# Start-up and step order of a fused FFT filter and gated FFN kernel: x on all partitions, interleaved filter rows, one table tensor, gated loads, written order, stages B and C in separate steps

## The chip, the core and the metric

The kernel runs on one core of one Trainium2 chip. The metric is the time of one execution in device microseconds (us). Three times of the kernel before were given: 1010.28, 1011.1 and 1007.79 us. Executions agree within about 0.3%, so an effect of 2 or 3 us is read only from several runs or from the trace itself.

## The reference

x is 8 batches of 3008 rows of 256 values. Each batch gets a real FFT along its 3008 rows, a product with a complex filter and the inverse FFT. Then all 24064 rows go through an FFN.

```python
X = np.fft.rfft(x, axis=1)
y = np.fft.irfft(X * (filt_r + 1j * filt_i)[None], n=3008, axis=1)
y = y.reshape(24064, 256)
out = (np.maximum(y @ w_gate, 0) * (y @ w_val)) @ w_out      # d_ff = 1536
```

## The kernel before

3008 is split as 94 times 32. Each batch's FFT is done in three stages of matmuls, with a transposition through DRAM between them:

- Stage A: the 94-point transform, an fp32 matmul (psA), copied to asb and stored in a DRAM tensor Abuf.
- Stage B: Abuf is loaded as at; a 32-point transform (psX), two products with the filter on VectorE (tt, uu), the inverse 32-point transform (psD), copied to dsb and stored in Dbuf.
- Stage C: Dbuf is loaded as dC; the inverse 94-point transform (psY), copied to yT.

The FFN then works on blocks of 376 rows. A block has 12 steps (ft 0 to 11). A step does four matmuls of 376 columns (psV, psG), ScalarE copies psV (vsb), VectorE multiplies (prod), and three matmuls of 256 columns (psO) use the products of the block before. FFT stages of the next batch are put into FFN steps as "side" work, so that TensorE never stops. There psX, psD and psY share two buffers of the accumulation memory, called banks below. Only batch 0's FFT has no FFN beside it; this document calls that time the start-up, up to the first psV matmul. The rest, from the first psV matmul to the last psO matmul, is called the FFN phase.

The parts that the change touches (cuts are marked):

```python
def load_x(b, eng):
    for c in range(N2 // NC2):                       # 4 tiles of 94 partitions
        xf = sb.tile([N1, NC2 * D], FP32, tag="xf", bufs=4)
        for (p0, p1) in ((0, 80), (80, N1)):
            eng.dma_start(xf[p0:p1], ...)
...
def hold_gpsimd(tile_):                              # a gate: GpSimd's next loads wait for tile_
    scr = sb.tile([32, 8], BF16, tag="scr", bufs=1)
    nc.gpsimd.tensor_copy(scr, tile_)
...
nc.sync.dma_start(WA, ...); load_x(0, nc.sync)
load_filters(); load_tables(); load_vg(0)
warm(20)                                             # warm-up: matmuls on constants, result not used
for i, f in enumerate(items_a(0)):
    f(); warm(1)
    if i == 7: place_tables(0)
load_at(0); place_filters(0)
for i, f in enumerate(items_b(0, after)):            # after: at g == 10, gate, load_vg(1), load_vg(2)
    if i == 4: place_tables(H); place_filters(1)     # copies on VectorE
    f()
load_d(0); hold_gpsimd(dCs[0, 0][0:32, 0, 0:8]); load_o(); load_x(1, nc.gpsimd)
...
for i, f in enumerate(items_a(b + 1)): side.setdefault(20 + (3 * i) // 2, []).append(f)
side.setdefault(45, []).append(lambda b=b: load_at(b + 1))
side.setdefault(46, []).append(lambda b=b: load_x(b + 2, nc.gpsimd))
for i, f in enumerate(items_b(b + 1)): side.setdefault(56 + (7 * i) // 4, []).append(f)
side.setdefault(79, []).append(lambda b=b: load_d(b + 1))
...
if ft in (5, 8) and bi + 1 < len(blocks):            # stage C of the next block
    item_c(*blocks[bi + 1], 0 if ft == 5 else 1)
```

This is the order in which the program is written. The kernel before leaves the final order of each engine's instructions to a scheduler.

## Time and profile before

| | value | from |
|---|---|---|
| timed runs | 1007.79 to 1011.1 us | three runs |
| span of the profiled execution | 3590.8 us | page, first line |
| TensorE busy | 99% | page, part 1 |
| start of psV, psG, psO groups | every 1.25 us (2 x 376 or 3 x 256 columns) | timeline |

The profiled execution is 3.6 times as long as the timed ones. The page's head (span and instructions; then each engine's busy time, share and instructions):

```profile
span 3590.8 us, 18213 instructions
...
PE 3561.6 (99%) x6756; PEld 1532.6 (43%) x6756; DVE 601.8 (17%) x1062; ACT 581.3 (16%) x1177; POOL 48.5 (1%) x92
```

And three neighbouring groups of the timeline (start, busy time, engine and line, operation, output and inputs, count):

```profile
1010.34 1.57 PE L326 MATMUL psV<-yT,WvT 128*128 128x376 bf16 x2
...
1011.59 1.57 PE L326 MATMUL psG<-yT,WgT 128*128 128x376 bf16 x2
...
1012.85 1.42 PE L346 MATMUL psO<-WoT,prod 128*128 128x256 bf16 x3
```

Two matmuls of 376 columns take 1.25 us from start to start, and three of 256 take 1.26 us. That is about 600 columns per microsecond. TensorE's rate should be 2400 by the Trainium skill (TensorE: Matmul & The Clock Gate, Part 1), so this one execution ran at about a quarter of it, though the granted clock is given as 1.00. (The trace of this execution holds no entry for the clock at all; so the 1.00 means only that nothing was recorded.) On such a slow TensorE all other engines look idle, and almost every wait is hidden. This profile can be used for durations on the other engines and for orders, but not for the balance of the timed runs. A second thing can be read from it: GpSimd's queue issues all six loads of gate and value weights from 30.2 to 34.5 us, and the copy that was meant to gate the last four comes at 119 us. The scheduler has put the loads before their gate. The first of the four:

```profile
31.65 0.72 POOL L202 DMA_DIRECT2D WvT<-in_moe_w_val_dram  x1
```

And the copy, further on in the same timeline:

```profile
118.94 0.18 POOL L214 COPY scr<-dsb 32x8 bf16<-32x8 bf16 x1 [73.39 <-ACT dsb L279]
```

VectorE's costs are read from the groups of the same page: 550 ns for one prod, 692 for a tt and 681 for a uu.

### The profile page before, as it was taken

What the parts mean: (1) busy time and instruction counts of PE and PEld (TensorE: products, weight loads), DVE (VectorE), ACT (ScalarE), POOL (GpSimd) and SP (SyncE); (2) the same over time, 40 slices, a digit from 0 to 9 for tenths busy, and PEclk for the clock granted to TensorE, in tenths of its full rate; (3) what the DMA queues carried; (4) which work ended last, traced back from release to release, by engine and by line L of the source; (5) the groups of instructions that cost most, each with busy time, mean ns of one, the idle gap of its engine ahead of it and who ended that gap; (6) DMA issues with size and microseconds to landing.
All of it is one profiled execution on the core that took longest, in us unless ns stands there. A gap on an engine that the chain in (4) does not pass through costs nothing.

```text
span 3590.8 us, 18213 instructions
## 1 busy us (share of the span) xinstructions
PE 3561.6 (99%) x6756; PEld 1532.6 (43%) x6756; DVE 601.8 (17%) x1062; ACT 581.3 (16%) x1177; POOL 48.5 (1%) x92
## 2 busy tenths in 40 slices
PE   8899999999999999999999999999999999999999
PEld 2333444344443344433444344443444434444444
DVE  2311221112211121111211112110121101211111
ACT  0111111111111111111111111111111111111111
POOL 2000000000000000000000000000000000000000
DMA  6302010110101101001010110101101001010000
GB/s 113 83 21 62 16 33 9 33 49 16 32 9 33 49 17 35 9 30 49 19 33 9 32 51 19 31 7 40 43 19 31 9 18 29 19 31 9 9 9 13
DMA packets 95226, 105.94 MB, mean 30 GB/s; under 512 B 5920, under 2 KB 85984, under 8 KB 92128
## 3 DMA queue, kind: packets, MB, share of 16 engines
q1 hardware_dynamic: 83984, 78.11, 7.5%
q0 software_dynamic: 10176, 25.47, 3.0%
q10 hardware_dynamic: 976, 1.20, 0.2%
q8 instruction: 53, 0.87, 0.1%
q14 instruction: 37, 0.30, 0.0%
HBM read 58.84 MB, written 49.81 MB: 30 GB/s over the span
## 4 chain that ended last, share of the span: by engine, by line
PE 99%; DMA 1%; ACT 0%; DVE 0%; issue 0%; SPq 0%
PE psO L346 26%; PE psV L326 26%; PE psG L326 26%; PE psA L230 12%; PE psX L263 2%; PE psD L277 2%; PE psD L276 2%; PE psY L309 2%; PE psJ L369 1%; DMA xf<-in_x_dram 0%; DMA dC<-Dbuf_74 0%; DMA at<-Abuf_66 0%; DMA WA<-dft_wa 0%; DMA Abuf_66<-asb 0%; DMA Dbuf_74<-dsb 0%; DVE asb L234 0%
## 5 line engine op out<-in xcount | busy, mean ns | idle before, releaser
L346 PE MATMUL psO<-WoT,prod 128*128 128x256 bf16 (+1 forms) x2304 | 1162.4, 692 | 0.0
L326 PE MATMUL psV<-yT,WvT 128*128 128x376 bf16 x1536 | 1144.3, 887 | 0.0
L326 PE MATMUL psG<-yT,WgT 128*128 128x376 bf16 x1536 | 1143.3, 883 | 0.0
L331 DVE SCALAR_TENSOR_TENSOR prod<-psG,vsb 128x376 bf16<-128x376 f32 x768 | 422.1, 550 | 2606.2 <-PE psG L326 2604.2
L346 PEld LDWEIGHTS <-prod 128*128 128x128 bf16 (+1 forms) x2304 | 533.8, 232 | 703.2 <-issue 675.6
L329 ACT CAST vsb<-psV 128x376 bf16<-128x376 f32 x768 | 362.7, 472 | 1630.3 <-PE psV L326 1630.3
L326 PEld LDWEIGHTS <-WgT 128*128 128x128 bf16 x1536 | 341.2, 222 | 584.1 <-issue 584.1
L326 PEld LDWEIGHTS <-WvT 128*128 128x128 bf16 x1536 | 332.1, 221 | 433.8 <-issue 418.2
L230 PE MATMUL psA<-xf,WA 94*96 94x512 f32 x256 | 455.9, 1927 | 11.5 <-DMA xf<-in_x_dram 11.5
L236 ACT CAST asb<-psA 96x512 bf16<-96x512 f32 x120 | 69.8, 582 | 635.5 <-PE psA L230 635.5
L309 PEld LDWEIGHTS <-dC 96*128 96x128 bf16 x512 | 95.2, 216 | 119.6 <-issue 107.9
L277 PE MATMUL psD<-uu,I2u 128*128 128x256 bf16 x192 | 134.3, 699 | 0.0
L276 PE MATMUL psD<-tt,I2t 128*128 128x256 bf16 x192 | 134.0, 698 | 0.0
L230 PEld LDWEIGHTS psA<-xf,WA 94*96 94x96 f32 x256 | 102.6, 413 | 61.5 <-issue 43.0
L309 PE MATMUL psY<-M_83,dC 96*128 96x94 bf16 x512 | 113.4, 425 | 7.1 <-DMA dC<-Dbuf_74 7.1
L279 ACT CAST dsb<-psD 128x512 bf16<-128x512 f32 x96 | 56.3, 586 | 360.5 <-PE psD L277 360.5
L263 PE MATMUL psX<-at,F_84 128*128 128x256 bf16 x192 | 105.1, 692 | 7.3 <-DMA at<-Abuf_66 7.3
L351 ACT COPY osb<-psO 128x512 f32<-128x512 f32 (+1 forms) x128 | 61.3, 479 | 261.3 <-PE psO L346 261.3
L266 DVE TENSOR_TENSOR tt<-psX,Ftr 128x512 bf16<-128x512 f32 x96 | 66.4, 692 | 147.6 <-PE psX L263 139.1
L267 DVE TENSOR_TENSOR uu<-psX,Fti 128x512 bf16<-128x512 f32 x96 | 65.4, 681 | 0.0
L141 POOL DMA_DIRECT2D xf<-in_x_dram x56 | 29.8, 537 | 2390.6 <-PE psA L230 2389.7
L263 PEld LDWEIGHTS <-F_84 128*128 128x128 bf16 x192 | 40.7, 212 | 48.9 <-issue 34.9
(38 smaller groups left out, 236.2 us busy)
## 6 DMA issues: line engine op xcount, KB each, us to landing
xf<-in_x_dram POOLq DMA_DIRECT2D x28, 640.0 KB, 5.5
out_dram<-osb SPq DMA_DIRECT2D x64, 256.0 KB, 2.2
out_dram<-osb SPq DMA_DIRECT2D x64, 120.0 KB
xf<-in_x_dram POOLq DMA_DIRECT2D x28, 112.0 KB, 5.9
xf<-in_x_dram SPq DMA_DIRECT2D x4, 640.0 KB, 10.5
Abuf_66<-asb SPq DMA_DIRECT2D x4, 384.0 KB, 4.4
at<-Abuf_66 SPq DMA_DIRECT2D x4, 384.0 KB, 4.5
Dbuf_74<-dsb SPq DMA_DIRECT2D x4, 384.0 KB, 3.4
```

The source lines that it names most:

```text
L230: nc.tensor.matmul(psA[0:NROW], WA, xf[:, j * 512:(j + 1) * 512], start=True, stop=True)
L236: nc.scalar.copy(dst, psA[0:NROW])
L263: nc.tensor.matmul(psX[:, i], F2[:, g + i, :], at[:, g + i, :], start=True, stop=True)
L266: nc.vector.tensor_tensor(tt, psX, Ftr[:, g:g + 2, :], op=ALU.mult)
L267: nc.vector.tensor_tensor(uu, psX, Fti[:, g:g + 2, :], op=ALU.mult)
L276: nc.tensor.matmul(psD[:, i], I2t[:, g + i, :], tt[:, i], start=True, stop=False)
L277: nc.tensor.matmul(psD[:, i], I2u[:, g + i, :], uu[:, i], start=False, stop=True)
L309: nc.tensor.matmul(psY[:, j * N1:(j + 1) * N1], dCs[b, z // 2][:, (z % 2) * 4 + j, h * 128:(h + 1) * 128], M1, start=True, stop=True)
L326: nc.tensor.matmul(pt[:, :W], w[:, h, ft * 128:(ft + 1) * 128], yt[:, h, :], start=(h == 0), stop=(h == 1))
L329: nc.scalar.copy(vsb, psV[:, :W])
L331: nc.vector.scalar_tensor_tensor(prod, in0=psG[:, :W], scalar=0.0, in1=vsb, op0=ALU.max, op1=ALU.mult)
L346: nc.tensor.matmul(psO[:tw, t % 2], prods[ft][:, t * 128:t * 128 + tw], WoT[:, ft, :], start=(ft == 0), stop=(ft == NFT - 1))
```

## The change

The intent: give x the DMA engines alone at the start and spread it over all partitions; load filters, tables and weights only when a gate opens; keep the written order so that the gates hold; take copies off VectorE in the first stage B; shorten the last store and load before stage C; and keep stages B and C in different FFN steps. The diff, cut to its core:

```diff
+    ctx.enter_context(tc.manual_schedule())          # each engine keeps the written order
-    WA = consts.tile([N1, NROW], FP32)
+    WA = consts.tile([128, NROW], FP32)              # row n1 on partition 4 * (n1 % 32) + n1 // 32
+    XF = [consts.tile([128, NX2 * D], FP32, name=f"XF{c}") for c in range(N2 // NX2)]   # NX2 = 16
...
     def load_x(b, eng):
-            for (p0, p1) in ((0, 80), (80, N1)):
-                eng.dma_start(xf[p0:p1], ...)
+            for m in range(3):
+                eng.dma_start(xf[m:m + 4 * rows - 3:4], ...)      # 32 rows, every fourth partition
...                                                    # filter rows: dst[r:r+31:2] and dst[r+1:r+32:2]
...                                                    # three tables in one tensor, two DMAs, issued in stage A
+                if half == 0: nc.vector.tensor_copy(dst[r + 32:r + 64, gs, :], dst[r:r + 32, gs, :])
+                else:         nc.sync.dma_start(dst[r + 32:r + 64, gs, :], dst[r:r + 32, gs, :])
...
+        cuts = (0, 6, 12, 18, 24) if b else (0, 6, 12, 18, 22, 24)   # stores of dsb
-                if g: inv()
+                if len(held) > 2: inv()                # tt, uu, dsb: 4 buffers
...                                                    # dC: eight loads of 4 columns, not four of 8
-    load_filters(); load_tables(); load_vg(0)
+    (zero XF on VectorE and GpSimd); load_x(0, nc.sync)
+    hold_gpsimd(XF[0][0:32, 0:8]); load_filters(0); load_filters(1)
+    warm(16)
+    (stage A, with load_tables() after its third item)
+    load_at(0); place_tables(0, nc.vector.tensor_copy); place_tables(1, nc.scalar.copy)
+    place_filters(0); place_filters(1)
+    hold_gpsimd(ats[0][0:32, NG - 1, 0:8]); load_vg(0); load_vg(1); load_vg(2)
+    (stage B with two warm-up matmuls per item); warm(16); load_d(0)
...
+            s0 = 5 if b else 20                        # side work: A at s0, at load at s0 + 25, x at s0 + 26
-                side.setdefault(56 + (7 * i) // 4, []).append(f)
+                at_step(s0 + 36 + (3 * i) // 2, f)
-            if ft in (5, 8) and bi + 1 < len(blocks):
+            if ft in (7, 10) and bi + 1 < len(blocks):
```

More of the change, by code (lines that the diff above doesn't have):

```diff
@@ L40, in _tables @@
     p = np.arange(16)
-    wa = np.zeros((N1, NROW))
+    wa = np.zeros((128, NROW))
+    part = 4 * (n1 % 32) + n1 // 32
     m1 = np.zeros((NROW, N1))
@@ L55, in _tables @@
         th = 2 * np.pi * ((n1 * k1) % N1) / N1
-        wa[:, 2 * hg] = np.cos(th)
+        wa[part, 2 * hg] = np.cos(th)
         if k1 not in (0, 47):
-            wa[:, 2 * hg + 1] = -np.sin(th)
+            wa[part, 2 * hg + 1] = -np.sin(th)
             m1[2 * hg] = 2.0 * np.cos(th) / S
             m1[2 * hg + 1] = -2.0 * np.sin(th) / S
-            k = np.concatenate([k1 + N1 * p, S - (N1 * (p + 1) - k1)])
-            conj = np.concatenate([np.ones(16), -np.ones(16)])
+            k = np.stack([k1 + N1 * p, S - (N1 * (p + 1) - k1)], 1).reshape(32)
+            conj = np.tile([1.0, -1.0], 16)
             th = 2 * np.pi * (np.outer(n2, k) % S) / S
@@ L72, in _tables @@
             c, s = np.cos(th), np.sin(th)
-            f[0:32, 0:16] = c
-            f[0:32, 32:48] = -s
-            t[0:16, 0:32] = 2.0 * c.T
-            t[32:48, 0:32] = -2.0 * s.T
-            u[0:16, 0:32] = -2.0 * s.T
-            u[32:48, 0:32] = -2.0 * c.T
+            f[0:32, 0:32:2] = c
+            f[0:32, 32::2] = -s
+            t[0:32:2, 0:32] = 2.0 * c.T
+            t[32::2, 0:32] = -2.0 * s.T
+            u[0:32:2, 0:32] = -2.0 * s.T
+            u[32::2, 0:32] = -2.0 * c.T
             if k1 == 0:
@@ L86, in _tables @@
         f2[rows, g], i2t[rows, g], i2u[rows, g] = f, t[:, perm], u[:, perm]
-    return (wa.astype(np.float32), m1.astype(NBF16), f2.astype(NBF16),
-            i2t.astype(NBF16), i2u.astype(NBF16))
+    tab = np.stack([f2, i2t, i2u], 1).reshape(128, 3, 2, NG // 2, 64).transpose(0, 2, 1, 3, 4)
+    return wa.astype(np.float32), m1.astype(NBF16), np.ascontiguousarray(tab).astype(NBF16)
 @with_exitstack
@@ L108 @@
     NC2 = 8
+    NX2 = 16
     NZ = 8
     W = S // NZ
-    wa_h, m1_h, f2_h, i2t_h, i2u_h = _tables()
+    wa_h, m1_h, tab_h = _tables()
+    ctx.enter_context(tc.manual_schedule())
     consts = ctx.enter_context(tc.tile_pool(name="consts", bufs=1))
@@ L131 @@
     WoT = consts.tile([128, NFT, D], BF16)
-    xfs = {}
     def load_x(b, eng):
-        for c in range(N2 // NC2):
-            xf = sb.tile([N1, NC2 * D], FP32, tag="xf", bufs=4)
-            w = NC2 * D
-            for (p0, p1) in ((0, 80), (80, N1)):
-                eng.dma_start(xf[p0:p1], _ap(x, b * S * D + p0 * N2 * D + c * w,
-                                             [[N2 * D, p1 - p0], [1, w]]))
-            xfs[b, c] = xf
+        for c, xf in enumerate(XF):
+            w = NX2 * D
+            for m in range(3):
+                rows = min(32, B * N1 - (b * N1 + 32 * m))
+                eng.dma_start(xf[m:m + 4 * rows - 3:4],
+                              _ap(x, (b * N1 + 32 * m) * N2 * D + c * w, [[N2 * D, rows], [1, w]]))
@@ L145 @@
     H = NG // 2
     FILT = ((filt_r, Ftr), (filt_i, Fti))
-    stgs = []
+    tabs = sb.tile([128, 2, 3, H, 64], BF16, tag="tabs", bufs=1)
     def load_tables():
-        for (nm, h, t) in (("f2", f2_h, F2), ("i2t", i2t_h, I2t), ("i2u", i2u_h, I2u)):
-            nc.vector.memset(t, 0.0)
-            stg = sb.tile([128, NG, 64], BF16, tag="stg", bufs=3)
-            stgs.append((t, stg, nc.inline_tensor(h, name="dft_" + nm).ap()))
-        for g0 in (0, H):
-            for (t, stg, src) in stgs:
-                nc.scalar.dma_start(stg[:, g0:g0 + H], src[:, g0:g0 + H])
+        src = nc.inline_tensor(tab_h, name="dft_tab").ap()
+        for half in range(2):
+            nc.scalar.dma_start(tabs[:, half], src[:, half])
@@ L157, in load_tables, with place_tables @@
         nc.scalar.dma_start(M1, nc.inline_tensor(m1_h, name="dft_m1").ap())
-    def place_tables(g0):
-        for (t, stg, src) in stgs:
+    def place_tables(half, copy):
+        for i, t in enumerate((F2, I2t, I2u)):
             for a in range(2):
                 r = slice(a * 64, a * 64 + 64)
-                nc.vector.tensor_copy(t[r, g0:g0 + H, a * 64:a * 64 + 64], stg[r, g0:g0 + H])
-    def load_filters():
-        for (src, dst) in FILT:
-            for g in (H - 1, NG - 1):
-                nc.vector.memset(dst[64:128, g, :], 0.0)
-        for half in range(2):
-            first = 2 - half
-            gl = H * half + H - 1
-            for fi, (src, dst) in enumerate(FILT):
-                for a in range(2):
-                    r = a * 64
-                    k1, n = first + 2 * a, H - a
-                    gs = slice(H * half, H * half + n)
-                    nc.gpsimd.dma_start(dst[r:r + 16, gs, :],
-                                        _ap(src, k1 * D, [[N1 * D, 16], [4 * D, n], [1, D]]))
-                    nc.gpsimd.dma_start(dst[r + 16:r + 32, gs, :],
-                                        _ap(src, (N1 - k1) * D, [[N1 * D, 16], [-4 * D, n], [1, D]]))
-                nc.gpsimd.dma_start(dst[64:80, gl, :], _ap(src, 47 * half * D, [[N1 * D, 16], [1, D]]))
-                if half == 0:
-                    nyq[fi] = sb.tile([1, D], BF16, tag="nyq", bufs=2, name="nyq")
-                    nc.gpsimd.dma_start(nyq[fi], _ap(src, (S // 2) * D, [[D, 1], [1, D]]))
@@ new lines, in place_tables, with load_filters @@
+                copy(t[r, half * H:half * H + H, a * 64:a * 64 + 64], tabs[r, half, i])
+    def load_filters(half):
+        first = 2 - half
+        for fi, (src, dst) in enumerate(FILT):
+            for a in range(2):
+                r = a * 64
+                k1, n = first + 2 * a, H - a
+                gs = slice(H * half, H * half + n)
+                nc.gpsimd.dma_start(dst[r:r + 31:2, gs, :],
+                                    _ap(src, k1 * D, [[N1 * D, 16], [4 * D, n], [1, D]]))
+                nc.gpsimd.dma_start(dst[r + 1:r + 32:2, gs, :],
+                                    _ap(src, (N1 - k1) * D, [[N1 * D, 16], [-4 * D, n], [1, D]]))
+        if half == 0:
+            for fi, (src, dst) in enumerate(FILT):
+                nc.gpsimd.dma_start(dst[64:95:2, H - 1::H, :],
+                                    _ap(src, 0, [[N1 * D, 16], [47 * D, 2], [1, D]]))
+                nyq[fi] = sb.tile([1, D], BF16, tag="nyq", bufs=2, name="nyq")
+                nc.gpsimd.dma_start(nyq[fi], _ap(src, (S // 2) * D, [[D, 1], [1, D]]))
@@ L194, in place_filters @@
                 r = a * 64
-                nc.vector.tensor_copy(dst[r + 32:r + 64, gs, :], dst[r:r + 32, gs, :])
+                if half == 0:
+                    nc.vector.tensor_copy(dst[r + 32:r + 64, gs, :], dst[r:r + 32, gs, :])
+                else:
+                    nc.sync.dma_start(dst[r + 32:r + 64, gs, :], dst[r:r + 32, gs, :])
             if half == 0:
@@ L211, in hold_gpsimd @@
     def hold_gpsimd(tile_):
-        scr = sb.tile([32, 8], BF16, tag="scr", bufs=1)
+        scr = sb.tile([32, 8], tile_.dtype, tag="scr", bufs=1)
         nc.gpsimd.tensor_copy(scr, tile_)
@@ L228, in one @@
             psA = ps.tile([128, 512], FP32, tag=fft_tag(), name="psA")
-            xf = xfs[b, c]
-            nc.tensor.matmul(psA[0:NROW], WA, xf[:, j * 512:(j + 1) * 512],
+            o = (c * NC2 % NX2) * D + j * 512
+            nc.tensor.matmul(psA[0:NROW], WA, XF[c * NC2 // NX2][:, o:o + 512],
                              start=True, stop=True)
@@ L252, in load_at, with items_b @@
                               _ap(Abuf[b], g0 * 128 * D, [[D, 128], [128 * D, GC], [1, D]]))
-    def items_b(b, after=lambda g, tile_: None):
+    def items_b(b, junk=0):
         held = []
         st = {}
+        cuts = (0, 6, 12, 18, 24) if b else (0, 6, 12, 18, 22, 24)
         def fwd(g):
@@ L263, in fwd @@
                 nc.tensor.matmul(psX[:, i], F2[:, g + i, :], at[:, g + i, :], start=True, stop=True)
-            tt = sb.tile([128, 2, D], BF16, tag="tt", bufs=3)
-            uu = sb.tile([128, 2, D], BF16, tag="uu", bufs=3)
+            tt = sb.tile([128, 2, D], BF16, tag="tt", bufs=4)
+            uu = sb.tile([128, 2, D], BF16, tag="uu", bufs=4)
             nc.vector.tensor_tensor(tt, psX, Ftr[:, g:g + 2, :], op=ALU.mult)
@@ L271, in inv @@
             g, tt, uu = held.pop(0)
-            if g % GC == 0:
-                st["dsb"] = sb.tile([128, GC, D], BF16, tag="dsb", bufs=2, name="dsb")
+            if g in cuts:
+                st["dsb"] = sb.tile([128, GC, D], BF16, tag="dsb", bufs=4, name="dsb")
+                st["g"] = g
             psD = ps.tile([128, 2, D], FP32, tag=fft_tag(), name="psD")
@@ L277, in inv @@
                 nc.tensor.matmul(psD[:, i], I2u[:, g + i, :], uu[:, i], start=False, stop=True)
-            o = g % GC
+            o = g - st["g"]
             nc.scalar.copy(st["dsb"][:, o:o + 2, :], psD)
-            if o + 2 == GC:
-                nc.sync.dma_start(_ap(Dbuf[b], (g - o) * 128 * D, [[D, 128], [128 * D, GC], [1, D]]),
-                                  st["dsb"])
-                after(g, st["dsb"])
+            if g + 2 in cuts:
+                nc.sync.dma_start(_ap(Dbuf[b], st["g"] * 128 * D,
+                                      [[D, 128], [128 * D, o + 2], [1, D]]), st["dsb"][:, :o + 2, :])
         for g in range(0, NG, 2):
@@ L287, in both @@
                 fwd(g)
-                if g:
+                if junk:
+                    warm(junk)
+                if len(held) > 2:
                     inv()
@@ L291, in items_b @@
         yield inv
+        yield inv
     dCs = {}
     def load_d(b):
-        for z in range(0, N2, 8):
-            dC = sb.tile([NROW, 8, D], BF16, tag="dC", bufs=6)
-            nc.sync.dma_start(dC, _ap(Dbuf[b], z * D, [[N2 * D, NROW], [1, 8 * D]]))
-            dCs[b, z // 8] = dC
+        for z in range(NZ):
+            dC = sb.tile([NROW, 4, D], BF16, tag="dC", bufs=12)
+            nc.sync.dma_start(dC, _ap(Dbuf[b], z * 4 * D, [[N2 * D, NROW], [1, 4 * D]]))
+            dCs[b, z] = dC
     yTs = {}
@@ L309, in item_c @@
             nc.tensor.matmul(psY[:, j * N1:(j + 1) * N1],
-                             dCs[b, z // 2][:, (z % 2) * 4 + j, h * 128:(h + 1) * 128], M1,
+                             dCs[b, z][:, j, h * 128:(h + 1) * 128], M1,
                              start=True, stop=True)
@@ L354, in o_part @@
                               osb[:tw, :n])
-    nc.sync.dma_start(WA, nc.inline_tensor(wa_h, name="dft_wa").ap())
-    load_x(0, nc.sync)
-    load_filters()
-    load_tables()
-    load_vg(0)
     junk = sb.tile([128, 512], BF16, tag="junk", bufs=1)
-    nc.vector.memset(junk, 1.0)
     def warm(n):
@@ L369, in warm @@
             nc.tensor.matmul(psJ, junk[:, 0:128], junk, start=True, stop=True)
-    warm(20)
+    nc.vector.memset(junk, 1.0)
+    nc.sync.dma_start(WA, nc.inline_tensor(wa_h, name="dft_wa").ap())
+    nc.vector.memset(XF[0][:, :NX2 * D // 2], 0.0)
+    nc.gpsimd.memset(XF[0][:, NX2 * D // 2:], 0.0)
+    nc.vector.memset(XF[1][:, :NX2 * D // 2], 0.0)
+    nc.gpsimd.memset(XF[1][:, NX2 * D // 2:], 0.0)
+    load_x(0, nc.sync)
+    for t in (F2, I2t, I2u):
+        nc.vector.memset(t, 0.0)
+    for (src, dst) in FILT:
+        for g in (H - 1, NG - 1):
+            nc.vector.memset(dst[64:128, g, :], 0.0)
+    hold_gpsimd(XF[0][0:32, 0:8])
+    load_filters(0)
+    load_filters(1)
+    warm(16)
     for i, f in enumerate(items_a(0)):
@@ L374 @@
         warm(1)
-        if i == 7:
-            place_tables(0)
+        if i == 2:
+            load_tables()
     load_at(0)
+    place_tables(0, nc.vector.tensor_copy)
+    place_tables(1, nc.scalar.copy)
     place_filters(0)
-    def after(g, tile_):
-        if g == 10:
-            hold_gpsimd(tile_[0:32, 5, 0:8])
-            load_vg(1)
-            load_vg(2)
-    for i, f in enumerate(items_b(0, after)):
-        if i == 4:
-            place_tables(H)
-            place_filters(1)
+    place_filters(1)
+    hold_gpsimd(ats[0][0:32, NG - 1, 0:8])
+    for c in range(3):
+        load_vg(c)
+    for f in items_b(0, 2):
         f()
+    warm(16)
     load_d(0)
@@ L404, with at_step @@
             side = {}
+            def at_step(s, f):
+                side.setdefault(s, []).append(f)
+            s0 = 5 if b else 20
             for i, f in enumerate(items_a(b + 1)):
-                side.setdefault(20 + (3 * i) // 2, []).append(f)
-            side.setdefault(45, []).append(lambda b=b: load_at(b + 1))
+                at_step(s0 + (3 * i) // 2, f)
+            at_step(s0 + 25, lambda b=b: load_at(b + 1))
             if b + 2 < B:
-                side.setdefault(46, []).append(lambda b=b: load_x(b + 2, nc.gpsimd))
+                at_step(s0 + 26, lambda b=b: load_x(b + 2, nc.gpsimd))
             for i, f in enumerate(items_b(b + 1)):
-                side.setdefault(56 + (7 * i) // 4, []).append(f)
-            side.setdefault(79, []).append(lambda b=b: load_d(b + 1))
+                at_step(s0 + 36 + (3 * i) // 2, f)
+            at_step(s0 + 60, lambda b=b: load_d(b + 1))
         elif z == 0:
@@ L421 @@
                 f()
-            if ft in (5, 8) and bi + 1 < len(blocks):
-                item_c(*blocks[bi + 1], 0 if ft == 5 else 1)
+            if ft in (7, 10) and bi + 1 < len(blocks):
+                item_c(*blocks[bi + 1], 0 if ft == 7 else 1)
         prev = (blk, prods)
```

## The prediction

> **What bounds the kernel now.** The page's busy shares (PE 99%, DVE 17%, ACT 16%) come from an execution of 3590.8 us, against timed runs of 1010.28 us. In the timeline one 512-column bf16 matmul starts every 0.84 us, about 610 columns/us, though the clock column says 1.00. So it ran TensorE at about a quarter speed and hides shorter waits. The Trainium skill (TensorE: Matmul & The Clock Gate, terms and HAM trace caveats) gives 2.4 GHz and reports the gate seen stuck at K=1/4; the trace agrees with the rate. I scale.
>
> Counting the groups view's matmuls by columns (fp32 as four passes, since two instructions take 1.68 us each in the timeline): FFN 1.745 M, psA 0.262 M, psX+psD 0.147 M, psY 0.048 M, warm-up 0.018 M, together 2.22 M, 925 us at 2.4 GHz; about 940 with a few ns per matmul. After the first FFN matmul some 913 us of it remain. The other ~95 us are start-up (no FFN yet), the tail (about 3 us) and stalls in the FFN phase.
>
> **Start-up before, estimated at full clock.** The first x tile lands at 11.5 us; TensorE then does 22 warm-up matmuls before stage A goes on. x packets end at 24 us, because tables and filters share the DMA engines (DMA by time). Weight loads, issued at 30-34 us ahead of the gates written for them, fill the engines to 47 us (about 190 GB/s) just when stage A's write and stage B's read need them. DVE evictions of stage A stand behind filter copies that wait for the second filter half. My sum: A ends ~36, B starts ~47, B is DVE-bound (tt and uu start every 0.60 us, so 1.2 us x 12), then store 3.4 us, load 5.0 us and C: FFN starts near 74 us.
>
> **Start-up after.** x waits for memsets (a 1536-word one took 1.34 us, so +2 to 3 us), then has the engines alone and reaches all partitions; the skill (SBUF — State Buffer, Door 1: The DMA port swizzle) says bandwidth follows the ports that the partitions reach. Warm-up runs during that load. A is TensorE-bound, 16 x (0.85+0.21) us, about 10 to 27 us; round trip to 34-35; B to ~51; shorter final stores and loads; FFN near 58-60. Gain about 14 us, all critical.
>
> **FFN phase.** A step costs TensorE ~0.96 us, a stage-B item 0.65 more; DVE needs 0.46 for prod plus 1.2 for tt/uu. psX, psD and psY share two banks. With psY in the same step as B it must wait for uu: about 1.1 us, once per batch. Removed: -7 us. But items come every 1.5 steps instead of 1.75; more adjacent pairs make psX wait ~0.2 us for the bank: +4 us. Earlier FFT stages (5 instead of 20) and eight smaller dC loads remove waits for dC, if there are any: -3 us. Two banks limit what deeper lookahead gives. In sum -4 to -10 us.
>
> **Prediction:** 987 us, eight in ten between 968 and 1002; faster by over 2%: 0.62, within 2%: 0.36, slower: 0.02.
>
> **What would show it right:** the chain of waits and the timeline: x landed before ~17 us, no weight packets before stage A's round trip ends, first psG matmul 10-18 us earlier; in the FFN phase, psY steps without TensorE idle time, psX gaps of at most 0.3 us.
>
> **What would make it wrong:** if start-up before was already ~60 us, the gain halves; if filters, now gated behind x, land after 35 us, B starts late; if the FFN-phase excess is weight-load cost of small psY matmuls (94 columns against 128-column loads) and not waits, the phase stays unchanged; if denser B items fall behind on DVE, it gets longer.

## The result, and the profile after

The changed kernel took 992.28 us (median of four, 991.98 to 992.85), the kernel before 1009.34 us (median of four, 1007.79 to 1011.1). The ratio is 0.9831, with a 95% interval of 0.9812 to 0.985. The change made the kernel 1.7% faster, which is within 2%.

The new profile was taken at full clock. To have a profile of the kernel before at full clock as well, the unchanged kernel was run once more (before_again below: 1007.92 us). The page's head and the share of TensorE by slice, before_again first:

```profile
span 1006.2 us, 18213 instructions
...
PE 958.2 (95%) x6756; PEld 658.8 (65%) x6756; DVE 584.6 (58%) x1062; ACT 548.0 (54%) x1177; POOL 50.0 (5%) x92
...
PEclk9877999999999999999999999999999999999999
```

and the same lines of the page of after:

```profile
span 991.1 us, 18249 instructions
...
PE 963.2 (97%) x6789; PEld 662.9 (67%) x6792; DVE 581.3 (59%) x1054; ACT 552.9 (56%) x1183; POOL 42.8 (4%) x79
...
PEclk9789999999999999999999999999999999999999
```

The start-up in the timeline of before_again (start us, us, engine, line, operation, and in brackets the idle time before it and what ended it):

```profile
11.90 3.73 PE L230 MATMUL psA<-xf,WA 94*96 94x512 f32 x4 [11.90 <-DMA xf<-in_x_dram]
...
15.42 5.66 PE L369 MATMUL psJ<-junk 128*128 128x512 bf16 x22
...
36.91 3.60 PE L230 MATMUL psA<-xf,WA 94*96 94x512 f32 x8
...
47.57 7.24 SPq L251 DMA_DIRECT2D at<-Abuf  x4
...
56.03 1.46 PE L263 MATMUL psX<-at,F 128*128 128x256 bf16 x6 [15.53 <-DMA at<-Abuf]
...
61.59 0.95 DVE L195 COPY Fti<-Fti 32x3072 bf16<-32x3072 bf16 x1
```

and further on in the same view:

```profile
79.29 1.73 SPq L298 DMA_DIRECT2D dC<-Dbuf  x4
...
83.22 1.04 PE L309 MATMUL psY<-M,dC 96*128 96x94 bf16 x11 [10.45 <-DMA dC<-Dbuf]
...
84.27 0.47 PE L326 MATMUL psV<-yT,WvT 128*128 128x376 bf16 x1
```

The same places of after:

```profile
11.43 1.99 PE L228 MATMUL psA<-XF_85,WA 128*96 128x512 f32 x2 [4.97 <-DMA XF_85<-in_x_dram]
...
30.91 1.02 PE L228 MATMUL psA<-XF_86,WA 128*96 128x512 f32 x2
...
35.86 2.40 SPq L249 DMA_DIRECT2D at<-Abuf_68  x4
...
39.29 0.58 PE L262 MATMUL psX<-at,F_88 128*128 128x256 bf16 x2 [7.15 <-DVE Fti L195]
...
44.92 0.76 POOL L200 DMA_DIRECT2D WvT<-in_moe_w_val_dram  x1 [0.29 <-issue]
```

and further on:

```profile
61.93 3.60 SPq L300 DMA_DIRECT2D dC<-Dbuf_76  x8
...
64.63 0.81 PE L311 MATMUL psY<-M_87,dC 96*128 96x94 bf16 x8 [4.89 <-DMA dC<-Dbuf_76]
...
65.68 0.86 PE L328 MATMUL psV<-yT,WvT 128*128 128x376 bf16 x2 [0.25 <-ACT yT L317]
```

The first FFN matmul starts at 65.7 us instead of 84.3, a gain of 18.6 us. Stage A (first to last psA) shrank from 28.0 to 19.9 us, the way from A to B from 16.1 to 8.0 us. Stage B (first psX to last psD) stayed at 16.5 and 16.7 us, and the rest went from 11.8 to 9.7 us. TensorE waited 15.5 us for at before; after, it waits 7.1 us. The profile puts this down to VectorE's last filter copy, which ended at 39.23 us; but the first tile of at had landed only 0.1 us before (at 39.16), so both limits stand there.

Two things in the start-up before are the scheduler's doing. It put 22 warm-up matmuls behind the first four instructions of stage A (15.42 us above), where they take 5.5 us of stage A; after runs its 16 warm-up matmuls from 1.46 us on, before x has landed. And it moved the copies of tables and filters, which the source has in the middle of stage B, to earlier times, all but one (61.59 us above). So stage B took no more time before than it takes after.

The FFN phase, on the other hand, became longer: 918.3 us before, 921.9 us after (last psO start minus first psV start, in the two traces). 18.6 minus 3.6 is the 15.0 us by which the profiled spans differ (1006.2 and 991.1 us; 0.1 is rounding and tail). The waits of TensorE in before_again (who waited for whom, us in total, times, longest):

```profile
PE psX L263 <- DMA at<-Abuf: 15.5, 1, 15.5
...
PE psY L309 <- DMA dC<-Dbuf: 10.4, 1, 10.4
PE psD L277 <- DVE uu L267: 2.5, 8, 0.3
```

and in after:

```profile
PE psX L262 <- DVE Fti L195: 7.1, 1, 7.1
...
PE psY L311 <- DMA dC<-Dbuf_76: 4.9, 1, 4.9
PE psD L276 <- DVE uu L266: 2.6, 13, 0.2
```

What is left in the FFN phase is small on both sides. Matmuls of 376, 256 and 94 columns start every 159, 109 and 41 ns (medians of the after trace). The gaps beyond these medians, added up where one is over 30 ns and the clock is full (from 89 us in before_again, from 72 us in after), make 2.5 us before and 6.8 us after. (The phase grew by less than these 4.3 us; it begins at half clock in both, for 4.3 us before and 3.4 us after, from the start of psV to 88.6 and 69.1 us.) Of the 6.8 us, 5.4 us stand between a psX and the psD after it.

### The profile page after: what moved, and what is told of

It is laid out like the page before. It is cut to its first block, busy times and chain, and to the rows that moved or that the text cites. A ratio compares the mean times of both kernels' runs of the same rounds, so it can differ in the third digit from the quotient of the medians.

```text
span 991.1 us, 18249 instructions
## 1 busy us (share of the span) xinstructions
PE 963.2 (97%) x6789; PEld 662.9 (67%) x6792; DVE 581.3 (59%) x1054; ACT 552.9 (56%) x1183; POOL 42.8 (4%) x79
## 4 chain that ended last, share of the span: by engine, by line
PE 91%; DVE 3%; DMA 3%; ACT 1%; issue 1%; SPq 0%; ACTq 0%; DVEq 0%
PE psO L348 24%; PE psV L328 24%; PE psG L328 24%; PE psA L228 11%; PE psY L311 2%; PE psD L276 2%; PE psD L277 2%; PE psX L262 1%; DMA Dbuf_76<-dsb 1%; DVE uu L266 1%; DMA Abuf_68<-asb 1%; DVE tt L265 1%; DMA XF_85<-in_x_dram 1%; ACT yT L317 1%; ACT vsb L331 1%
## 5 line engine op out<-in xcount | busy, mean ns | idle before, releaser
L348 PE MATMUL psO<-WoT,prod 128*128 128x256 bf16 (+1 forms) x2304 | 375.0, 273 | 0.0
L328 PE MATMUL psV<-yT,WvT 128*128 128x376 bf16 x1536 | 371.5, 323 | 0.5 <-ACT yT L317 0.2
L328 PE MATMUL psG<-yT,WgT 128*128 128x376 bf16 x1536 | 370.6, 323 | 0.0
L348 PEld LDWEIGHTS <-prod 128*128 128x128 bf16 (+1 forms) x2304 | 246.1, 110 | 89.9
L328 PEld LDWEIGHTS <-WgT 128*128 128x128 bf16 x1536 | 150.1, 98 | 96.0 <-issue 1.5
L328 PEld LDWEIGHTS <-WvT 128*128 128x128 bf16 x1536 | 143.6, 98 | 79.6 <-issue 68.0
L279 ACT CAST dsb<-psD 128x512 bf16<-128x512 f32 x96 | 56.2, 586 | 68.9 <-PE psD L277 65.8
L228 PE MATMUL psA<-XF_85,WA 128*96 128x512 f32 x128 | 66.8, 603 | 5.0 <-DMA XF_85<-in_x_dram 5.0
L228 PE MATMUL psA<-XF_86,WA 128*96 128x512 f32 x128 | 65.4, 592 | 1.6 <-ACT asb L234 1.6
L265 DVE TENSOR_TENSOR tt<-psX,Ftr 128x512 bf16<-128x512 f32 x96 | 65.4, 681 | 1.7 <-PE psX L262 1.7
L266 DVE TENSOR_TENSOR uu<-psX,Fti 128x512 bf16<-128x512 f32 x96 | 65.4, 681 | 0.0
L276 PE MATMUL psD<-tt,I2t 128*128 128x256 bf16 x192 | 47.4, 273 | 3.3 <-DVE uu L266 2.6
L277 PE MATMUL psD<-uu,I2u 128*128 128x256 bf16 x192 | 47.4, 273 | 0.3 <-DVE uu L266 0.3
L311 PE MATMUL psY<-M_87,dC 96*128 96x94 bf16 x512 | 42.7, 206 | 4.9 <-DMA dC<-Dbuf_76 4.9
```

Source lines behind the costliest of these rows:

```text
L228: nc.tensor.matmul(psA[0:NROW], WA, XF[c * NC2 // NX2][:, o:o + 512], start=True, stop=True)
L265: nc.vector.tensor_tensor(tt, psX, Ftr[:, g:g + 2, :], op=ALU.mult)
L266: nc.vector.tensor_tensor(uu, psX, Fti[:, g:g + 2, :], op=ALU.mult)
L276: nc.tensor.matmul(psD[:, i], I2t[:, g + i, :], tt[:, i], start=True, stop=False)
L277: nc.tensor.matmul(psD[:, i], I2u[:, g + i, :], uu[:, i], start=False, stop=True)
L311: nc.tensor.matmul(psY[:, j * N1:(j + 1) * N1], dCs[b, z][:, j, h * 128:(h + 1) * 128], M1, start=True, stop=True)
```

## The experiments

All outputs are right. "FFN start" is the first psV matmul and "FFN phase" is as above, both read from the run's profile. Kernels that share the whole start-up code (after, after_old_steps, after_c_at_4) differ by 1.1 us in FFN start, so differences of that size in start-up are not read. The experiments ran in three groups on three chips, each beside the kernel before (medians of 1008.01 to 1009.02 us there, 1009.34 in the result), but after was not run again with them. A difference to after of less than about 1.5 us of time is therefore not read.

| kernel | FFN start us | FFN phase us | profiled span us | median us (range, runs) | ratio to before (95%) |
|---|---|---|---|---|---|
| before_again | 84.3 | 918.3 | 1006.2 | 1007.92 (1) | |
| after | 65.7 | 921.9 | 991.1 | 992.28 (991.98-992.85, 4) | 0.9831 (0.9812-0.985) |
| after_old_steps | 64.7 | 925.7 | 994.0 | 996.81 (996.13-999.85, 5) | 0.9888 (0.9873-0.9904) |
| before_new_steps | 84.7 | 921.3 | 1009.4 | 1010.65 (1009.27-1011.79, 6) | 1.0019 (1.0005-1.0033) |
| after_more_bufs | 64.3 | 921.9 | 989.8 | 991.88 (991.43-992.92, 4) | 0.9836 (0.9822-0.985) |
| after_no_gates | 75.1 | 920.1 | 998.8 | 999.97 (999.3-1001.53, 5) | 0.9921 (0.9909-0.9932) |
| before_written_order | 75.9 | 928.0 | 1007.5 | 1009.56 (1009.32-1009.69, 5) | 1.0013 (1.0001-1.0025) |
| after_scheduler | 77.5 | 919.4 | 1000.4 | 1002.31 (1001.5-1005.15, 5) | 0.9946 (0.9933-0.9959) |
| after_plain_x | 64.8 | 928.7 | 997.1 | 1000.4 (998.88-1003.17, 6) | 0.9927 (0.9914-0.994) |
| after_c_at_4 | 65.8 | 921.8 | 991.2 | 993.09 (991.41-993.85, 4) | 0.9846 (0.9831-0.9861) |
| after_dve_copies | 69.6 | 920.2 | 993.7 | 994.74 (993.68-996.35, 4) | 0.9864 (0.9847-0.9881) |
| after_plain_filters | 63.8 | 921.6 | 988.9 | 992.61 (990.71-994.52, 4) | 0.9843 (0.9825-0.9861) |
| best | 65.4 | 919.7 | 988.6 | 989.02 (987.42-990.42, 4) | 0.9807 (0.9793-0.9822) |

### before_again: where was the time before?

The kernel is unchanged. The theory of the prediction splits the gain between start-up and FFN phase; one rival puts all of it in start-up, the other all in the FFN phase.

> The kernel before, unchanged, for a profile at full TensorE clock (its first profile ran at a quarter of it). After's first FFN matmul starts at 65.7 us and its FFN phase lasts 922.5 us. Split theory (my prediction): first FFN matmul here near 74 us, FFN phase near 930 us. Rival 1, all of the 17 us is start-up: first FFN matmul near 82 us, phase 922 to 924 us. Rival 2, all is FFN phase: first FFN matmul near 66 us, phase near 939 us with psY and psX waits on TensorE of over 10 us in sum.

First FFN matmul at 84.3 us, phase 918.3 us. Both are beyond what even rival 1 asked for: start-up gained more than the whole, and the FFN phase gave 3.6 us back. The prediction's 74 us for the start-up before was 10 us short. Its own sum had A end at about 36 and B start at about 47; the trace has the end of the last psA at 40.5 and the first psX at 56.0.

### after_old_steps and before_new_steps: the FFN steps alone

```diff
 # after_old_steps, from after
-            s0 = 5 if b else 20
+            s0 = 20
-                at_step(s0 + 36 + (3 * i) // 2, f)
+                at_step(s0 + 36 + (7 * i) // 4, f)
-            if ft in (7, 10) and bi + 1 < len(blocks):
+            if ft in (5, 8) and bi + 1 < len(blocks):
```

before_new_steps is the opposite: the kernel before, under its scheduler, with s0, the step numbers and the ft pair of after.

> After with the step numbers of before (first FFT step always 20, stage B every 1.75 steps, stage C at ft 5 and 8). Split theory: 4 to 10 us slower than after (996 to 1002 us), with one psY wait of about 1 us per batch on TensorE. Rival 1 (all start-up): within 2 us of after. Rival 2 (all FFN phase): near 1009 us.

> Before, still under the scheduler, with the step numbers of after alone. Split theory: 4 to 10 us faster than before. Rival 1 (all start-up): within 2 us of before. Rival 2: near 992 us.

In written order the old steps cost 3.8 us of FFN phase and 4.5 us of median time, as the split theory had it. Two waits per batch come back; the waits of TensorE in after_old_steps:

```profile
PE psY L311 <- ACT dsb L279: 4.7, 7, 0.7
...
PE psX L262 <- DVE uu L266: 3.6, 7, 0.5
```

From start to start, psY comes 0.84 us late in each of seven batches. (It waits for ScalarE's copy of the psD of the same step, not for uu as the prediction had it.) But in the kernel before, with the very same step numbers, this wait is 0.09 us: the scheduler has put psY between the psO matmuls, where it hardly has to wait. The timeline of before_again shows psO x1, psY x4, psO x2:

```profile
287.71 0.27 PE L346 MATMUL psO<-WoT,prod 128*120 128x256 bf16 x1
...
287.91 0.33 PE L309 MATMUL psY<-M,dC 96*128 96x94 bf16 x4
...
288.07 0.40 PE L346 MATMUL psO<-WoT,prod 128*120 128x256 bf16 x2
```

So the mechanism that the new steps remove was not there before. Under the scheduler the new steps even cost 3.0 us of FFN phase (1.7 us of median, 0.2% by the ratio). The new steps are the price and the repair of the written order; they are not a gain over the kernel before.

### after_more_bufs: are the waits for stores the cause of the rest?

```diff
-    asb bufs=2, dsb bufs=4, dC bufs=12
+    asb bufs=4, dsb bufs=5, dC bufs=11
```

> After with asb 4 instead of 2 buffers and dsb 5 instead of 4 (dC 11 instead of 12, to fit). After's trace shows evictions of stage A waiting 5.8 us for an Abuf store and the last dsb waiting 2.7 us for a Dbuf store. If these waits are what kept start-up from the predicted 58 to 60 us: first FFN matmul at 59 to 62 us and 4 to 6 us faster than after. Rival: the stores are late because the DMA engines are full, so the waits only move to the next load; then at most 2 us faster.

First FFN matmul 1.4 us earlier, hardly more than the scatter of 1.1, and the median 0.4 us lower. That fits the rival in size. In the trace stage A's evictions no longer wait for a store, and yet the first Abuf store takes 9.2 us from issue to landing (8.8 us in after) and the way from A to B stays at 8.0 us. That full DMA engines make the stores late fits this, but no run shows it alone.

### after_no_gates, before_written_order, after_scheduler: gates and order

```diff
 # after_no_gates, from after (written order kept)
-    hold_gpsimd(XF[0][0:32, 0:8])
+    load_tables()
     load_filters(0); load_filters(1)
+    load_vg(0); load_vg(1); load_vg(2); load_o()
...                                     # no gates on ats and dCs, and no loads there
 # before_written_order, from before
+    ctx.enter_context(tc.manual_schedule())
 # after_scheduler, from after
-    ctx.enter_context(tc.manual_schedule())
```

> After, still in written order, with its gates taken away: tables issued at the start, filters not held for x, gate, value and output weights and batch 1's x not held, as the scheduler has them in the kernel before. Gate theory: the start-up gain (first FFN matmul at 84.3 us before, 65.7 us after) is the weight, output-weight and x(1) transfers kept out of stage A's store and stage B's load; expected first FFN matmul at 78 to 84 us, FFN phase 922 us as in after, time 1004 to 1010 us. Rival (layouts and shorter chains gave it, gates little): first FFN matmul below 71 us, time below 997 us.

> Before with the one line that keeps instructions in written order, so that its own gates (weights 1 and 2 after the second Dbuf store, output weights and batch 1's x after dC) hold. Gate theory: first FFN matmul at 70 to 75 us instead of 84.3. In the FFN phase the written order brings back the psY wait of 0.84 us and the psX wait of 0.68 us per batch seen in after_old_steps: phase 925 to 928 us instead of 918.3. Sum: 1000 to 1006 us. Rival (written order worth nothing by itself): 1007 to 1012 us.

> After without the line that keeps the written order: the instruction order shows the gate copies behind the loads they should hold. Gate theory: first FFN matmul at 76 to 84 us, FFN phase 919 to 922 us, time 1000 to 1008 us. Rival (layouts and tables gave the start-up): first FFN matmul below 71 us, time 990 to 995 us.

Without gates, FFN start is 75.1 us: later than in after by 9.4 us, about half of the 18.6. That lies between what the two theories had asked for. Stage A itself is as short as in after (18.3 us), so it isn't the gates that shorten A. The written order alone does so in the kernel before (28.0 to 17.4 us in before_written_order, where the warm-up matmuls come before x); but after_scheduler has 21.9 us without it, so the rest of the change shortens A too. The loss stands in one wait:

```profile
PE psX L262 <- DMA at<-Abuf: 20.9, 1, 20.9
```

In after this wait is 7.1 us. Of the 13.8 us between them about 4.5 come back elsewhere: stage A is 1.6 us shorter, and the way from stage B to the first FFN matmul 2.9 us. Which of the held loads costs most was not tried; the first tile of at landed at 51.85 us, just after batch 1's x (51.6 us). In before_again the same wait is 15.5 us, and the transfers in it are visible. In its 32 to 56 us the issue list has, besides at and Abuf, weights and output weights and the first tile of batch 1's x; columns are size and median us from issue to landing:

```profile
at<-Abuf SPq DMA_DIRECT2D x4, 384.0 KB, 9.3
...
WgT<-in_moe_w_gate_dram POOLq DMA_DIRECT2D x3, 256.0 KB, 9.3
WoT<-in_moe_w_out_dram POOLq DMA_DIRECT2D x2, 384.0 KB, 13.6
...
xf<-in_x_dram POOLq DMA_DIRECT2D x1, 640.0 KB, 15.9
```

The same of after, in its 32 to 40 us:

```profile
at<-Abuf_68 SPq DMA_DIRECT2D x4, 384.0 KB, 4.9
```

at needs 9.3 us to land in before_again, and 4.9 us in after, where only stage A's last store and two copies of filter rows run beside it. The loads are on GpSimd's queue and at is on SyncE's, which doesn't help. The Trainium skill says so (DMA: Bandwidth & Descriptors, Issuing engines are not separate DMA queues): all queues run on the same 16 engines and interleave. This trace agrees.

The line for the written order, added to the kernel before, moved FFN start from 84.3 to 75.9 us and the FFN phase from 918.3 to 928.0 us, so that nothing came of it (ratio 1.0013). Its expectation missed the sum by 4 us: the phase was at the top of the range, and FFN start just beyond it. Taken away from after, the same line costs 11.8 us of FFN start and gives 2.5 us of FFN phase back. The written order is good where the program's author knows what the scheduler does not, namely which loads must stay behind; it is bad where the scheduler had filled waits by itself. One such place is the first stage B: with the line alone it lasts 22.2 us instead of 16.5, because the copies of tables and filters are back in its middle.

### after_plain_x: x on 94 adjacent partitions

```diff
-    WA = consts.tile([128, NROW], FP32); four memsets of XF
+    WA = consts.tile([N1, NROW], FP32)
-            for m in range(3):  ... xf[m:m + 4 * rows - 3:4]
+            for (p0, p1) in ((0, 80), (80, N1)):  ... xf[p0:p1]
```

> After with x on partitions 0 to 93 in two DMAs of 80 and 14 rows, WA on the same 94, and so without the four memsets. Port theory (the prediction's): x packets move at about 350 GB/s in after; here at 240 or less, x lands 3 to 5 us later, but starts 2.5 us earlier; stage A is bound by TensorE and by its stores, so first FFN matmul within 2 us of after's 65.7, time within 2 us of after. Rival (spread x is a main part of the gain): 4 us or more slower than after.

FFN start is 64.8 us, so for the start-up the layout is worth nothing: slower transfers are made up by their earlier start (x is issued at 1.1 us here, and at 3.6 in after, behind the memsets). (In 4 to 12 us the issue list of after moves 307 GB/s, in 2 to 14 us that of after_plain_x 223 GB/s.) But the median went up by 8.1 us, and the FFN phase by 6.8 us, where neither the prediction nor this expectation looked. There x of a later batch is loaded while stage A's last store and stage B's load run. The issue list of after_plain_x (over the whole run, KB, median us to landing):

```profile
XF<-in_x_dram POOLq DMA_DIRECT2D x14, 1280.0 KB, 8.8
...
Abuf<-asb SPq DMA_DIRECT2D x32, 384.0 KB, 7.9
```

the issue list of after:

```profile
XF_85<-in_x_dram POOLq DMA_DIRECT2D x20, 512.0 KB, 6.3
...
Abuf_69<-asb SPq DMA_DIRECT2D x4, 384.0 KB, 4.0
```

and the wait of TensorE in after_plain_x:

```profile
PE psX L261 <- DMA at<-Abuf: 12.6, 7, 7.7
```

In batch 2 the last store of Abuf is issued at 225.2 us and the load that waits for it at 235.8 us, 10.6 us later; in after it is 5.2 us (224.6 and 229.9 us). TensorE waits for at 7.7 us in the start-up and then once in each of six batches, together 4.9 of the 6.8 us. (The seventh has no x load beside it, and there the 10.6 us are 3.1.) The skill's rule on ports (SBUF — State Buffer, Door 1) fits the two rates: the rate rises with the ports that a transfer's partitions reach. What counts, though, is less x's own landing than what it does to the small store next to it. This experiment keeps after's rows of 16 KB; the kernel before had rows of 8 KB on the same partitions, and its Abuf stores landed in 5.6 us. That suggests that the larger rows on few partitions are the problem and that the spread made them usable; rows of 8 KB were not tried in after, so it is not shown.

### after_c_at_4: what is the 5.4 us between psX and psD?

```diff
-            if ft in (7, 10) and bi + 1 < len(blocks):
-                item_c(*blocks[bi + 1], 0 if ft == 7 else 1)
+            if ft in (4, 10) and bi + 1 < len(blocks):
+                item_c(*blocks[bi + 1], 0 if ft == 4 else 1)
```

> After with stage C at ft 4 and 10 instead of 7 and 10 (steps that stage B leaves free too). Trace of after: at ft 7 ScalarE has the psO eviction (0.59 us) and C's first yT copy (0.48 us) in a row; the next vsb, prod and uu come late, and psD one step on waits 0.3 to 0.4 us for that uu. ScalarE-pile-up theory: the psX to psD waits fall from 5.4 us to below 2 us, the FFN phase from 922 to 917-919 us, time 3 to 5 us below after. Rival (the waits come from two B items in adjacent steps and the two shared banks, as the prediction has it): waits stay at 5 us or more, time within 1 us of after.

In after's timeline psD (243.40) starts when the uu of the step before (242.67, 0.68 us) has ended:

```profile
242.67 0.68 DVE L266 TENSOR_TENSOR uu<-psX,Fti 128x512 bf16<-128x512 f32 x1
...
242.86 0.38 PE L262 MATMUL psX<-at,F_88 128*128 128x256 bf16 x2
...
243.40 0.27 PE L276 MATMUL psD<-tt,I2t 128*128 128x256 bf16 x1 [0.16 <-DVE uu L266]
```

In after_c_at_4 the sum between psX and psD is 5.4 us as before: step 57 improved from 0.39 to 0.19 us, step 45 got worse from 0.32 to 0.47. The FFN phase is 921.8 us. The theory that C's copy on ScalarE causes the sum falls. The prediction's reading, two stage-B items in adjacent steps on two shared banks, isn't enough either: each of the last six batches has five pairs of steps with a psX and a psD in both, and in after only the two whose second step is 45 or 57 wait by more than 0.04 us. Both are steps with ft 9, two steps after ScalarE copies psO out at ft 7, which this run left in place. Whether that copy is the cause was not tried, so the cause stays open.

### after_dve_copies: copies in the first stage B

```diff
-    place_tables(1, nc.scalar.copy); place_filters(1)      # the latter by DMA
+    (at item 4 of stage B) place_tables(1, nc.vector.tensor_copy); place_filters(1)   # on VectorE
```

> After with the second half of tables and filter rows copied by VectorE in the middle of the first stage B, as before does, instead of by ScalarE and by DMA. In before_written_order these copies take 6.0 us of VectorE there and stage B lasts 22 us against 16.7. Theory (VectorE bounds the first stage B): stage B ends 5 to 6 us later, first FFN matmul at 70 to 72 us, time 4 to 6 us above after. Rival (the copies hide behind waits for DMA, and their DMA traffic was the cost): within 1.5 us of after.

VectorE does copies from 46.2 to 52.6 us, and TensorE waits for the next tt:

```profile
48.41 2.23 DVE L190 COPY Ftr<-Ftr 32x3072 bf16<-32x3072 bf16 x2
50.67 1.93 DVE L190 COPY Fti<-Fti 32x3072 bf16<-32x3072 bf16 x2
...
53.39 0.40 PE L273 MATMUL psD<-tt,I2t 128*128 128x256 bf16 x1 [4.76 <-DVE tt L262]
```

Stage B ends 6.9 us later (62.9 instead of 56.0 us), FFN start moves by 3.9 us and the time by 2.5 us. The direction is right and the size about half. The stores of the earlier groups land during the longer stage B, so the wait for dC falls from 4.9 to 2.1 us; and TensorE, with a shorter pause before psY, runs the first FFN steps at full clock (1.00 from 69.6 us on). This is a gain over the written order with the copies in it, not over the kernel before, whose scheduler had moved these copies out of stage B.

### after_plain_filters: filter rows not interleaved

```diff
-                nc.gpsimd.dma_start(dst[r:r + 31:2, gs, :], ...)
-                nc.gpsimd.dma_start(dst[r + 1:r + 32:2, gs, :], ...)
+                nc.gpsimd.dma_start(dst[r:r + 16, gs, :], ...)
+                nc.gpsimd.dma_start(dst[r + 16:r + 32, gs, :], ...)    # and the tables to match
```

> After with filter rows not interleaved: rows k on 16 adjacent partitions, mirrored rows on the next 16, tables to match. Theory (filter transfers are many 512-byte packets, bound by the engines and not by the ports, and the second half isn't on the critical chain): within 1.5 us of after, first FFN matmul within 1.5 us of 65.7. Rival (ports count here too, as they did for x): filters land over 3 us later and time 2 us or more above after.

Median 992.61 us against 992.28: the interleaving is worth nothing here (FFN start 63.8 us in the profile, if anything earlier by 1.9). Spreading over partitions helped x's rate, and did not help these loads: the last filter row landed at 31.5 us here and at 31.7 in after.

### best: a version that beats both

```diff
 # from after
+    C at ft 4 and 10; asb bufs=4, dsb bufs=5, dC bufs=11
-    warm(16)
+    warm(36)
     load_d(0)
```

> After with C at ft 4 and 10, asb 4 and dsb 5 buffers, and 36 warm-up matmuls instead of 16 before stage C, so that TensorE isn't idle for 5 us and cold in the first FFN steps (clock 0.66 in 60 to 70 us). Expected: 4 us from the steps, 1 from the buffers, 1.5 from the clock, so 985 to 988 us. If the ScalarE theory of after_c_at_4 falls: 989 to 991 us.

989.02 us (987.42 to 990.42), below all runs of after and of after_c_at_4; the latter ran beside it. (Whether it is over 2% faster than the kernel before is unclear: its interval holds 0.98.) The stretch of 66 to 72 us (PE, PEld, DVE, ACT, POOL busy, clock, DMA share, GB/s), in after:

```profile
66.00:72.00 6.00, 6.00 (x29) 3.22 (x28) 3.17 (x7) 3.07 (x7) 3.92 (x7) 0.74 1.04 209
```

and in best:

```profile
66.00:72.00 6.00, 6.00 (x42) 3.65 (x41) 4.50 (x9) 4.63 (x10) 3.87 (x7) 1.00 1.16 207
```

In after TensorE stands still for 4.9 us before psY, and its clock is 0.74 in the first FFN steps; with 20 more warm-up matmuls in that pause it is 1.00, and the FFN phase falls from 921.9 to 919.7 us. The other edits of best left the phase unchanged in the runs that tried them (921.9 us in after_more_bufs, 921.8 in after_c_at_4), so the warm-up is what remains, though it was not run alone. The skill (TensorE: Matmul & The Clock Gate, What's actually happening) puts the return to full clock at about 3.4 us of sustained work. After's trace is near it: TensorE starts again with psY at 64.63 us and with psV at 65.68, and pairs of matmuls take 0.63 us until 68.85 and 0.32 us from 69.31 on, 4.7 and 3.6 us later.

## Why the prediction was right or wrong

The time was right: 987 us with a range of 968 to 1002 was predicted, 992.28 us measured, and "within 2%" came true where 0.62 had been given to "faster by over 2%". The two terms behind it were each off, in opposite directions: the start-up gained 4.6 us more than predicted, and the FFN phase lost 3.6 us instead of gaining 4 to 10. That the number came out within 6 us is in part luck.

- "So it ran TensorE at about a quarter speed": right. The full-clock profile has 159 ns where the first had 627 (1.25 us for two). (The 2.4 GHz that it takes from the skill stand in the page's Part 1, not in its Terms.)
- "Start-up ... FFN starts near 74 us": too short by 10 us (84.3). Two steps failed. "A ends ~36" was 40.5 us, and from there to B, 11 us in the prediction, it took 15.5 us, so that "B starts ~47" was 56.0. The contention was named correctly (weights and x(1) on the engines), but its size wasn't.
- "Start-up after ... FFN near 58-60": too short by 6 us (65.7). The step that failed is A, "about 10 to 27 us": it ran from 11.4 to 31.9 us. Its 20.5 us are 3.4 more than 16 times 1.07 us: the first two groups ran at a clock of 0.52 (11 to 14 us), after TensorE had stood still for 5 us between warm-up and x, and the groups waited for an Abuf store that took 8.8 us to land while filters and tables were loading. The round trip itself, 7.4 us, and stage B were of the predicted length. From B's end (56.3) to the first FFN matmul it took 9.4 us, where 7 to 9 were predicted; the weights, gated until stage B, landed until 58.8 us, and the first Dbuf store took 10.7 us from its issue at 47.6. More buffers don't cure this (after_more_bufs).
- "Gain about 14 us, all critical": 18.6 us. By stage, 8.1 us are in A, 8.1 between A and B, 2.1 after B, and 0.5 before the first psA; stage B gave nothing. About half is the gates, which act between A and B (after_no_gates, 9.4 us): here the mechanism was right. In A it was right too, since the prediction names the 22 warm-up matmuls in the middle and the evictions behind filter copies; the trace has 5.5 and 2.4 us for them, but no run takes them out alone. The 3.9 us of after_dve_copies are no part of the 18.6, as its section says. How the rest divides among smaller last stores, loads and tables was not tried one by one.
- "the skill ... says bandwidth follows the ports": right for the rate, wrong for the place. It gained nothing in start-up and 6.8 us in the FFN phase (after_plain_x), as a repair of the 16 KB rows.
- "psY in the same step as B ... Removed: -7 us": this is the step that failed in sign. The kernel before didn't pay it (0.09 us a batch), because its scheduler had moved psY. In written order it exists (0.84 us a batch), and the change removes a cost that it would itself have brought in.
- "adjacent pairs make psX wait ~0.2 us for the bank: +4 us": right in size only, 5.4 us. It is psD that waits, for uu and not for a bank, and only in two pairs of a batch; psX waits 0.12 us a batch.
- "remove waits for dC, if there are any: -3 us": there were none in the FFN phase of before_again.
- In sum "-4 to -10 us" for the FFN phase became +3.6 us. The fear that "small psY matmuls" pay for weight loads was wrong: they start every 41 ns.

Of the signs that the prediction gave beforehand, most came true: x had landed at 15.5 us, the first weights were issued at 44.9 us, after the round trip, psY has no wait in the FFN phase, and psX one of 0.39 us and otherwise 0.08 at most. The first psG came 18.2 us earlier, just beyond the 10 to 18.

## What to carry to other kernels

Look for a change's gain in each phase by itself, and have both profiles at the same clock before costing anything; here a gain of 18.6 us and a loss of 3.6 us look like one gain of 15. When a scheduler orders the instructions, read the order it made and not the source: it had undone the gates and put warm-up matmuls into stage A, and it had also already cured the wait that the new step numbers cure and moved the copies out of stage B. And cost a bulk load by what it does to the small store and load on the critical chain beside it, not by its own landing time.

## What the Trainium skill lacked or had wrong

- TensorE: Matmul & The Clock Gate, Back-to-back issue gap: it gives about 81 ns per matmul at 128 columns and 131 ns at 512 for streams of weight loads and matmuls. Here 94 columns, each with its own weight load of 128 columns, start every 41 ns; 376 columns every 159 ns; and the 36 warm-up matmuls of 512 columns before stage C in best every 216 ns. The page's simple formula, columns over 2.4 plus 2.5 ns, fits all three; its "sustained" figures don't.
- Same page, Part 1: it says that the gate's share is only a half or full (13/16 when three cores of a die are busy), and in a caveat that its events are unreliable and that it was seen stuck at a quarter for over 50 us. Here a whole execution of 3590.8 us ran at about 600 columns per us, with no entry for the clock in its trace. A sentence that this can hold for a whole profile, and that start-to-start times tell, would help.
- SBUF — State Buffer, Door 1: right for x's rate; for small strided loads the page has only the general remark of its next section, on size. Interleaving the filter rows (loads of 88 and 96 KB in packets of about 500 bytes) changed the time by 0.3 us, within the scatter.
- DMA: Bandwidth & Descriptors: it says that queues share the engines, not how much a bulk load delays a small one. Here a 384 KB store took 10.6 us instead of 5.2 us from its issue to the load behind it, depending only on how the x load beside it was laid out.
- No page has a time for GpSimd's memset (for VectorE's, VectorE: DVE Perf Modes has a rule in cycles): 128 x 2048 fp32 took 1.81 us on GpSimd and 1.76 us on VectorE in after, so the two share such work evenly.
